# A two-stage kernel (attention, then a capacity mixture of experts): first steps reordered, row stores held for the next norm, and the seventh expert's list moved up

## The chip, the cores and the metric

The kernel runs on one core of a Trainium2 chip. The metric is device time in microseconds (us) of one execution, the median of several runs. The profile is one execution recorded by the hardware profiler; its engines are PE (TensorE's matmuls, with PEld for its weight loads), DVE (VectorE), ACT (ScalarE), POOL (GpSimd) and SP (SyncE, which issues most transfers).

## The reference

Eight batches of eight heads, 576 positions, head size 64. Heads 0 to 3 look at the last 32 positions, heads 4 to 7 at every 32nd. The rows of all heads side by side are the tokens of a mixture of eight experts, each of which takes at most 576 tokens: the pairs (token, expert) are served from the largest logit down.

```python
scores = scale * np.matmul(q, k.transpose(0, 1, 3, 2))
masks = np.stack([mask_local if h < H // 2 else mask_strided for h in range(H)], axis=0)
scores = np.where(masks[None, :, :, :], scores, -1000000000.0)
attn = np.exp(scores - np.max(scores, axis=-1, keepdims=True))
attn = attn / (np.sum(attn, axis=-1, keepdims=True) + 1e-09)
x = np.matmul(attn, v)                      # (B, H, S, D) -> x: (4608, 512)
logits = x @ w_gate                         # (4608, 8)
for idx in np.argsort(-logits.flatten()):   # largest first
    tok, e = (int(idx) // E, int(idx) % E)
    if assigned[tok] >= 0 or counts[e] >= cap:
        continue
    assigned[tok] = e
    counts[e] += 1
for e in range(E):
    mask = assigned == e
    out[mask] = np.maximum(x[mask] @ w1[e], 0.0) @ w2[e]
```

## The kernel before

**Attention.** Work is cut into 16 units: for each batch one with the four strided heads (even units) and one with the four local heads (odd units). A unit has two parts, of two heads each, and each part is one step, so there are 32 steps, i = 0 to 31. In the body of the loop over i, step i finishes the scores of the part behind it (`close_scores`), turns the rows of the part before it (`turn`), multiplies the part's own weights by the values in two halves (`mix(p, 0)`, `mix(p, 1)`, 36 or 24 matmuls each) into the one accumulator `po`, opens the scores of the part after next (`open_scores`), scales its rows (`norm`), and shifts and exponentiates the scores of the next part (`shift`). Between the two halves stands `max_t`, which turns the maxima and makes `dd` on DVE. The order of the lines is the order on each engine: this stage has no scheduler, and every engine serves its queue strictly in order.

Local units need their values twice, shifted by 32 rows: `copy_v` copies rows in SBUF, six copies a unit. `square_v` sums the squares of a batch's values on ACT; `total_v` (a matmul with `twos` and a sum on DVE) and `scale_v` make of it a power of two by which rows are scaled in `norm`. For the first unit the scale comes too late, so `rescale` applies it afterwards.

Loads go out on SP through `flow`: a load waits for the third last one before it, or for a mark (a unit's `top` or its last norm, `done`). `load_kq` brings the keys and queries of one part, `load_v` half of a unit's values. `store` writes a unit's rows to `x_scr` in DRAM, one unit and a half behind; strided units use six transfers, three on SP and three on POOL.

**Experts.** A search on DVE and PE finds each expert's threshold in turn (`side`). For expert number ph (0 to 7), `weights` loads w1 and w2, sums their squares (`jk`, L990) and splits them into two halves of 16 bits (w1h, w1l, w2h, w2l, L1008 and L1009); `slots` numbers its tokens; `close` and `take` remove them from the logits, and prepare the next search (`point`); `fetch` makes the list of its rows: one-hot rows on DVE (`ohh`, `ohl`, `rv`), 36 small matmuls (L951), two more (L959), `idx`, then five gathers on POOL (`xr`, L1068), halving on ACT and DVE (`xg`) and five transposes by transfer (`xt`, L1059). `ffn` runs the first layer (192 matmuls of 288 columns, L1163), then the second in tiles of 128 tokens, the first, the tail tile of 64 (L1205) and three more (L1211). Each tile's rows are written by an indirect transfer on POOL (L1222).

Here PE's order is written by a clock of estimated costs: `chains` holds generators that say how long to wait before their next piece, and pieces are issued among the matmuls when the clock reaches their time. For the other engines a scheduler orders by priority; `urgent` raises it. `HURRY` names the experts whose one-hot rows are urgent, `T_HOT` is the wait between these rows and the 36 matmuls, `T_F` one ahead of a list.

## Time and profile before

| | |
|---|---|
| median of 3 runs | 682.43 us (677.96 to 693.18) |
| the profiled execution | 682.75 us, span 681.0 us |
| PE busy | 603.8 us, 89% of the span |
| DVE busy | 459.7 us, 68% |
| ACT busy | 330.9 us, 49% |
| POOL busy | 112.4 us, 16% |
| mean granted TensorE clock | 0.958 of full |
| moved by transfers | 102.40 MB, mean 150 GB/s |

The share of busy time is an average over stages with different limits: attention until about 190 us, the first search until about 225, then the experts. A busy PE is not PE at its peak, since matmuls overlap in the record: in a row of 24 matmuls at full rate each shows more than the distance to the next one. Idle time of an engine counts only where that engine is waited for.

### The profile page before, as it was taken

Reading aid. Unit: us, or ns where it says so; the run is one execution under the profiler, and the core shown is the slowest. Engines: PE = TensorE matmul, PEld = TensorE weight load, DVE = VectorE, ACT = ScalarE, POOL = GpSimd, SP = SyncE. Lnnn points to the kernel's source line nnn. Section 1 sums busy time; section 2 is a strip of 40 time slices with the busy share of each in tenths; the row PEclk is TensorE's granted clock in tenths of the full one; section 3 lists DMA queues with packets and bytes.
Section 4 is the critical chain, followed back from the end, with each engine's and each line's share of the span. In section 5 each row is a group of like instructions: output and inputs, shape, how many; then the busy total and the mean of one; then the engine's idle time right before and its main releaser. Section 6 shows DMA issues by size and latency. Waiting matters only on the chain.

```text
span 681.0 us, 19420 instructions
## 1 busy us (share of the span) xinstructions
PE 603.8 (89%) x8125; PEld 396.3 (58%) x8128; DVE 459.7 (68%) x1388; ACT 330.9 (49%) x551; POOL 112.4 (16%) x124
## 2 busy tenths in 40 slices
PE   8799999898946699889989999989989996999993
PEld 4576766776633475476467458447537644746741
DVE  4767887787877887787686686787777746580200
ACT  2444664446302564843851771673574386771210
POOL 2011101111001100500420430240150041211011
PEclk9779999899976899999999999999999997999997
DMA  8968888787414505913930860870680386911010
GB/s 239 215 168 248 237 241 235 184 249 213 126 38 171 163 9 184 243 31 117 261 80 30 302 125 1 284 173 2 222 203 33 134 258 192 248 35 47 1 39 31
DMA packets 76363, 102.40 MB, mean 150 GB/s; under 512 B 41292, under 2 KB 49062, under 8 KB 75763
## 3 DMA queue, kind: packets, MB, share of 16 engines
q1 hardware_dynamic: 68195, 79.61, 41.4%
q0 software_dynamic: 7360, 21.15, 10.3%
q8 instruction: 64, 1.05, 0.7%
q10 hardware_dynamic: 720, 0.39, 0.2%
q14 instruction: 24, 0.20, 0.1%
HBM read 73.60 MB, written 18.87 MB: 136 GB/s over the span
## 4 chain that ended last, share of the span: by engine, by line
PE 22%; issue 14%; DVE 11%; DMA 10%; ACT 5%; POOL 4%; SPq 1%; POOLq 0%; DVEq 0%; ACTq 0%
PE ph L1163 17%; DMA w<-in_w_dram 6%; POOL xr L1068 2%; DMA xt<-xg 2%; DMA xr<-x_scr,idx 2%; PE ph L1211 2%; DVE w1l L1009 2%; POOL out_dram L1222 1%; ACT jk L990 1%; DVE w2l L1009 1%; DVE xg L1058 1%; ACT w1h L1008 1%; DVE hl L1171 1%; DVE cm L807 1%; ACT xg L1057 1%
## 5 line engine op out<-in xcount | busy, mean ns | idle before, releaser
L1163 PE MATMUL ph<-xt,w1h 128*128 128x288 f16 (+2 forms) x1024 | 177.7, 289 | 9.1 <-DMA xt<-xg 6.7
L1163 PEld LDWEIGHTS <-w1h 128*128 128x128 f16 x1024 | 97.4, 99 | 40.2 <-issue 7.7
L1163 PE MATMUL ph<-xt,w1l 128*128 128x288 f16 (+2 forms) x512 | 111.5, 288 | 0.0
L1222 POOL DMA_INDIRECT out_dram<-y,idx x40 | 50.6, 1265 | 332.0 <-ACT y L1221 304.8
L1211 PE MATMUL ph<-w2h,hh 128*128 128x512 f16 x256 | 97.0, 379 | 1.3 <-DVE hl L1171 1.3
L1170 ACT ACTIVATE hh<-ph 128x576 f16<-128x576 f32 (+2 forms) x72 | 42.7, 595 | 113.4 <-PE ph L1163 113.2
L990 ACT ACTIVATE jk<-w 128x1024 f16<-128x1024 f32 x64 | 67.5, 1054 | 61.3 <-DMA w<-in_w_dram 60.0
L1211 PE MATMUL ph<-w2h,hl 128*128 128x512 f16 x256 | 97.0, 379 | 0.0
L1211 PE MATMUL ph<-w2l,hh 128*128 128x512 f16 x256 | 96.9, 379 | 0.0
L1171 DVE SCALAR_TENSOR_TENSOR hl<-ph,hh 128x576 f16<-128x576 f32 (+2 forms) x72 | 49.5, 687 | 49.1 <-ACT hh L1170 49.1
L1211 PEld LDWEIGHTS <-hh 128*128 128x128 f16 x512 | 49.2, 98 | 57.2 <-issue 6.6
L1163 PEld LDWEIGHTS <-w1l 128*128 128x128 f16 x512 | 50.4, 99 | 14.1 <-issue 1.3
L374 ACT ACTIVATE pr<-spa 128x576 f32<-128x576 f32 x32 | 20.8, 651 | 63.2 <-PE spa L371 51.2
L1068 POOL DMA_INDIRECT xr<-x_scr,idx x40 | 41.8, 1046 | 54.9 <-DMA w<-in_w_dram 25.3
L1009 DVE SCALAR_TENSOR_TENSOR w1l<-w,w_sw,w1h 128x512 f16<-128x512 f32 x64 | 45.4, 744 | 6.4 <-ACT w1h L1008 6.4
L1009 DVE SCALAR_TENSOR_TENSOR w2l<-w,w_sw,w2h 128x512 f16<-128x512 f32 x64 | 46.4, 744 | 1.8 <-ACT w2h L1008 1.6
L1211 PEld LDWEIGHTS <-hl 128*128 128x128 f16 x256 | 24.9, 97 | 38.7 <-issue 13.4
L1008 ACT ACTIVATE w1h<-w,w_sw 128x512 f16<-128x512 f32 x64 | 42.4, 708 | 3.1 <-DVE w_sw L208 1.8
L1008 ACT ACTIVATE w2h<-w,w_sw 128x512 f16<-128x512 f32 x64 | 41.2, 710 | 5.7 <-DVE w_sw L208 5.7
L1221 ACT ACTIVATE y<-ph,so 128x512 f32<-128x512 f32 x32 | 21.8, 680 | 44.3 <-PE ph L1211 31.7
L425 POOL DMA_DIRECT2D x_scr<-xs x23 | 15.0, 659 | 161.0 <-DVE vsum L296 113.1
L1058 DVE TENSOR_TENSOR xg<-xr,xg 128x512 f16<-128x512 f32 (+1 forms) x37 | 25.3, 687 | 14.8 <-ACT xg L1057 14.6
(618 smaller groups left out, 932.5 us busy)
## 6 DMA issues: line engine op xcount, KB each, us to landing
w<-in_w_dram SPq DMA_DIRECT2D x64, 512.0 KB
kl<-in_kl_dram SPq DMA_DIRECT2D x16, 304.0 KB
v_s<-in_ns_dram SPq DMA_DIRECT2D x16, 292.5 KB
v_l<-in_nl_dram SPq DMA_DIRECT2D x16, 292.5 KB
ks<-in_ks_dram SPq DMA_DIRECT2D x16, 288.0 KB
qs<-in_qt_dram SPq DMA_DIRECT2D x16, 288.0 KB
ql<-in_qt_dram SPq DMA_DIRECT2D x16, 288.0 KB
x_scr<-xl SPq DMA_DIRECT2D x8, 512.0 KB
```

The source lines that it names most:

```text
L374: nc.scalar.activation(pr[:, :S].rearrange("k (h n) -> k h n", h=2), u.sp[p][:, :, :HS], AF.Exp, scale=0.125)
L990: nc.scalar.activation(jk, wf[:, c * n4:(c + 1) * n4].rearrange("p c f -> p (c f)"), AF.Square, scale=1.41422, accum_out=sq[:, c:c + 1])
L1008: nc.scalar.activation(hi[:, c, f], wf[:, c, f], AF.Copy, scale=s_)
L1009: nc.vector.scalar_tensor_tensor(lo[:, c, f], wf[:, c, f], s_, hi[:, c, f], op0=OP.mult, op1=OP.subtract)
L1058: nc.vector.tensor_tensor(xs[:, 1], xv, xs[:, 0], op=OP.subtract)
L1068: nc.gpsimd.indirect_dma_start(out=xr[:n], out_offset=None, in_=x_rows, in_offset=bass.IndirectOffsetOnAxis(ap=idx[:n, t:t + 1], axis=0))
L1163: nc.tensor.matmul(tile_[:, j, :w], wt[:, d, f * 128:(f + 1) * 128], xt[:, d // 2, xx, d % 2, c], start=(k == 0), stop=(k == 3 * DC - 1))
L1170: nc.scalar.activation(hv, src, AF.Relu)
L1171: nc.vector.scalar_tensor_tensor(lv, src, 0.0, hv, op0=OP.max, op1=OP.subtract)
L1211: nc.tensor.matmul(py, a[:, f, ts_], w[:, f], start=(k == 0), stop=(k == len(todo) - 1))
L1221: nc.scalar.activation(y, py, AF.Copy, scale=so[:, t:t + 1])
L1222: st = nc.gpsimd.indirect_dma_start(out=out_rows, out_offset=bass.IndirectOffsetOnAxis(ap=idx[:n, t:t + 1], axis=0), in_=y[:n], in_offset= ...
```

## The change

Four things are changed in attention. The three copies of unit 1 within the odd row blocks (`k % 2`) run on ACT instead of DVE. The Square of units 1 and 2 is issued behind the `shift` of steps 1 and 2, and `total_v` with `scale_v` of the first two batches stands between the two halves of the mix of steps 2 and 4, instead of behind the `shift` of steps 1 and 3; the copies and the Square of unit 3 and the `rescale` move behind the work of their step (`late`). The keys and queries of unit 2 are loaded ahead of its values, without marks. And the first SP store of a unit waits for the last norm of the next unit, as the POOL stores did before.

For the seventh expert (ph = 6) the one-hot rows are urgent, the list starts without `T_F` and its matmuls after 3200 instead of 4200 of the planner's nanoseconds, `close` comes 9000 later, and of `close` only the three pieces are run that the eighth expert needs, which takes all tokens that are left.

```diff
-HURRY = (0, 1, 7)
+HURRY = (0, 1, 6, 7)
+T_HOT6, T_CLOSE6 = 3200, 9000
@@ copy_v
-                if k % 2:
+                if k % 2 and u is todo[1]:
+                    nc.scalar.activation(vn[64:96, t], vn[32:64, t], AF.Copy)
+                elif k % 2:
@@ store
-                            if q is nc.gpsimd and u not in todo[-3:]:
+                            if (q is nc.gpsimd or SR * f + k == 0) and u not in todo[-3:]:
                                 wait_for(ins, todo[todo.index(u) + 1].done)
...
-                    nc.sync.dma_start(xs[:n, :4 * D].rearrange("(t q) f -> q t f", q=128), xo[:, :n // 128])
+                    ins = nc.sync.dma_start(xs[:n, :4 * D].rearrange("(t q) f -> q t f", q=128), xo[:, :n // 128])
+                    if u not in todo[-3:]:
+                        wait_for(ins, todo[todo.index(u) + 1].done)
@@ the tables of the steps
-        mids2, mids3 = {1: todo[1]}, {}
-        squares = {}
+        mids2, mids3 = {2: todo[1]}, {}
+        squares, behind = {}, {-1: todo[0].square_v}
...
-                squares.setdefault(1, []).append(u.square_v)
+                behind[1] = u.square_v
                 for p in range(2):
-                    drips.setdefault(2, []).append(lambda p=p: todo[0].rescale(p))
+                    late.setdefault(2, []).append(lambda p=p: todo[0].rescale(p))
...
-                        q, o = (late, -4) if j == 3 and k % 2 else (drips, COPY_AT[k])
+                        q, o = (late, -3) if j == 3 and k in (0, 1, 3, 5) else (drips, COPY_AT[k])
...
-                    squares.setdefault(2 * j - V_AT + 2, []).append(u.square_v)
+                    (late if j == 3 else squares).setdefault(2 * j - V_AT + 2, []).append(u.square_v)
@@ the first loads
-        for f in range(2):
-            todo[2].load_v(f)
+        for p in range(2):
+            todo[2].load_kq(p)
+            todo[2].load_v(p)
@@ the loop over the steps
+            if i in (2, 4):
+                mids2[i].total_v(b)
+                mids2[i].scale_v()
...
-            if i in mids2 and i > 1:
+            if i in mids2 and i > 4:
                 mids2[i].total_v(b)
             warm(i, 3)
-            if i == -1:
-                todo[0].square_v()
-            if i == 1:
-                todo[1].total_v(b)
-                todo[1].scale_v()
+            if i in behind:
+                behind[i]()
@@ indices, side
-        yield T_HOT1 if ph == 1 else T_HOT
+        yield T_HOT1 if ph == 1 else T_HOT6 if ph == E - 2 else T_HOT
...
-            chains.append([due_now() + (T_F if 1 < ph < E - 1 else 0), fetch(ph, slot, wts)])
+            chains.append([due_now() + (T_F if 1 < ph < E - 2 else 0), fetch(ph, slot, wts)])
+            if ph == E - 2:
+                yield T_CLOSE6
...
-                    for f in todo:
+                    for f in todo if ph < E - 2 else todo[:3]:
```

**VectorE in steps 1 and 2.** Before, from the maxima of unit 1's first part on (`mx_l_141`); `v_l_143` are unit 1's values, `mr`, `mh` and `dd` the chain from the maxima to the shift.

```order
L352 TENSOR_REDUCE mx_l_141<-spa 128x18
L324 COPY v_l_143<-v_l_143 32x780 x3
L361 TENSOR_REDUCE mr<-spa 64x32
L363 TENSOR_TENSOR mh<-mr 64x32
L364 TENSOR_TENSOR mh<-mr,mh 64x32
L366 TENSOR_TENSOR dd<-mh,bm 128x576
L404 TENSOR_SCALAR rc_407<-po 118x12
L407 RECIPROCAL rc_407<-rc_407 118x12
L409 TENSOR_TENSOR xs<-po,rc_407 118x2x6x64
L296 TENSOR_REDUCE vsum<-spb 128x1
```

After the change, from the same row on.

```order
L355 TENSOR_REDUCE mx_l_141<-spa 128x18
L364 TENSOR_REDUCE mr<-spa 64x32
L366 TENSOR_TENSOR mh<-mr 64x32
L367 TENSOR_TENSOR mh<-mr,mh 64x32
L369 TENSOR_TENSOR dd<-mh,bm 128x576
L407 TENSOR_SCALAR rc_404<-po 118x12
L410 RECIPROCAL rc_404<-rc_404 118x12
L412 TENSOR_TENSOR xs<-po,rc_404 118x2x6x64
L330 COPY v_l_143<-v_l_143 32x780 x2
L330 COPY v_l_143<-v_l_143 32x520
L355 TENSOR_REDUCE mx_l_145<-spa 128x18
```

The three copies of L324 have left the engine, and the six small operations on the batch's scale that began with `vsum` (L296) stand only behind the next part's `dd`.

**TensorE in step 2.** Before, from the second shift matmul of step 1 on; `twos` is the weight of `total_v`, `vsq_113` the sums of squares of the first batch, L391 the mix, L358 the turned maxima.

```order
L371 MATMUL spa<-dd,sel 128x288
L294 LDWEIGHTS twos
L294 MATMUL spb<-vsq_113,twos 128x2
L348 MATMUL spa<-ql,kl 64x32 x24
L391 MATMUL po<-v_l_143,pr_127 32x65 x18
L358 MATMUL spa<-ident,mx_l_145 32x64 x2
L391 MATMUL po<-v_l_143,pr_127 32x65 x18
```

After the change:

```order
L374 MATMUL spa<-dd,sel 128x288
L351 MATMUL spa<-ql,kl 64x32 x24
L394 MATMUL po<-v_l_143,pr_127 32x65 x18
L361 MATMUL spa<-ident,mx_l_145 32x64 x2
L295 LDWEIGHTS twos
L295 MATMUL spb<-vsq_113,twos 128x2
L394 MATMUL po<-v_l_143,pr_127 32x65 x18
```

The matmul of the total has gone from ahead of the scores and the mix into the middle of the mix, and the second half of the mix is queued behind it.

**GpSimd at the seventh expert.** Before: the gathers of the sixth expert's rows (`xr`), outputs, the gathers of the seventh, outputs.

```order
L1068 DMA xr<-x_scr,idx 128x512 x4
L1068 DMA xr<-x_scr,idx 64x512
L1222 DMA out_dram<-y,idx 4608x512 x5
L1068 DMA xr<-x_scr,idx 128x512 x4
L1068 DMA xr<-x_scr,idx 64x512
L1222 DMA out_dram<-y,idx 4608x512 x3
```

After the change:

```order
L1078 DMA xr<-x_scr,idx 128x512 x4
L1078 DMA xr<-x_scr,idx 64x512
L1234 DMA out_dram<-y,idx 4608x512 x4
L1078 DMA xr<-x_scr,idx 128x512 x4
L1078 DMA xr<-x_scr,idx 64x512
L1234 DMA out_dram<-y,idx 4608x512 x4
```

The seventh expert's gathers stand ahead of one output, that of the tail tile. On TensorE the 36 list matmuls of this expert stand behind four matmuls of the sixth expert's tail tile; before, they stood behind all 24 and eight of the next tile. The transposes and weight loads on SP keep their order but for the read of the eighth expert's number, which now stands behind the first transpose of the seventh.

## Rows read from the trace of the kernel before

**Rows 1.** Stretches: start:end, length, busy (instructions) of each engine, PEclk, DMA share, GB/s.

```profile
core 0: us, PE busy (x) PEld busy (x) DVE busy (x) ACT busy (x) POOL busy (x), PEclk, DMA share, GB/s
16.20:22.48 6.28, 4.18 (x138) 3.26 (x130) 5.22 (x17) 2.86 (x3) 0.00 (x0) 1.00 0.88 166
22.48:31.89 9.41, 6.70 (x139) 4.52 (x133) 8.11 (x22) 2.54 (x4) 0.00 (x0) 0.73 1.03 237
31.89:40.57 8.68, 7.11 (x147) 5.55 (x147) 3.84 (x11) 4.95 (x8) 2.18 (x3) 0.70 0.87 228
40.57:47.51 6.94, 6.94 (x153) 5.83 (x152) 4.25 (x15) 2.45 (x6) 0.00 (x0) 0.76 0.37 96
47.51:61.81 14.30, 13.80 (x425) 9.96 (x423) 11.58 (x31) 9.53 (x16) 0.56 (x1) 1.00 0.85 239
194.00:214.00 20.00, 10.63 (x224) 7.86 (x222) 15.69 (x66) 0.00 (x0) 0.00 (x0) 0.50 0.10 33
```

**Rows 2.** Timeline, steps 1, 2: start, length, engine, instruction; idle time before, and releaser.

```profile
17.61 1.51 DVE L324 COPY v_l<-v_l 32x780 f32<-32x780 f32 x3 [0.40 <-DMA v_l<-in_nl_dram]
...
19.29 2.12 ACT L291 ACTIVATE jk<-v_l 64x2304 f16<-64x2304 f32 x1 [3.14 <-DVE v_l L324]
...
20.35 0.41 PE L371 MATMUL spa<-dd,sel 128*128 128x288 bf16 x2 [1.13 <-DVE dd L366]
...
21.55 0.16 PE L294 MATMUL spb<-vsq,twos 128*128 128x2 bf16 x1 [0.80 <-ACT jk L291]
...
28.64 0.32 PE L348 MATMUL spa<-qs,ks 64*54 64x54 f32 x8 [1.59 <-DMA qs<-in_qt_dram]
```

**Rows 3.** Timeline of step 7: a unit's stores on SP and the next norm.

```profile
59.65 1.81 SPq L425 DMA_DIRECT2D x_scr<-xs  x3
...
60.13 0.82 DVE L409 TENSOR_TENSOR xl<-po,rc 128x640 f32<-128x640 f32 x1
```

**Rows 4.** Stretches where the seventh expert takes over.

```profile
540.00:550.00 10.00, 9.50 (x88) 4.54 (x86) 6.02 (x31) 7.07 (x13) 2.00 (x2) 1.00 0.97 349
550.00:560.00 10.00, 10.00 (x48) 4.51 (x46) 5.43 (x8) 8.38 (x14) 6.21 (x7) 1.00 0.76 211
562.54:567.85 5.31, 0.28 (x2) 0.10 (x2) 4.70 (x12) 4.45 (x9) 1.74 (x2) 0.84 0.94 220
567.85:573.20 5.35, 5.35 (x24) 3.32 (x25) 1.62 (x3) 0.63 (x2) 0.00 (x0) 0.52 0.88 348
```

**Rows 5.** Timeline: the rows of the sixth and the seventh expert.

```profile
500.61 7.58 SPq L1059 DMA_TRANSPOSE xt<-xg  x5
...
511.08 0.65 PE L1163 MATMUL ph<-xt,w1h 128*128 128x288 f16 x4
...
541.92 1.05 PE L1205 MATMUL ph<-w2h,hh 128*64 128x512 f16 x8
...
543.40 1.02 DVE L943 TENSOR_TENSOR ohl<-sh,iota 128x768 f16<-128x768 f16 x2
...
546.47 1.32 PE L951 MATMUL pr__8784<-ohl,rv 128*32 128x64 f16 x36
...
550.37 0.98 POOL L1068 DMA_INDIRECT xr<-x_scr,idx  x1 [0.31 <-issue]
...
555.99 7.99 SPq L1059 DMA_TRANSPOSE xt<-xg  x5
...
567.85 0.90 PE L1163 MATMUL ph<-xt,w1h 128*128 128x288 f16 x3 [4.11 <-DMA xt<-xg]
```

**Rows 6.** Timeline of the seventh expert's first layer: the eighth's list.

```profile
574.08 0.76 DVE L1171 SCALAR_TENSOR_TENSOR hl<-ph,hh 128x576 f16<-128x576 f32 x1 [4.61 <-ACT hh L1170]
...
580.25 1.51 PE L951 MATMUL pr__9136<-ohl,rv 128*32 128x64 f16 x36 [1.55 <-DVE rv L937]
```

**Rows 7.** The tile `xr`, 545 to 575: from issue to landing, five gathers.

```profile
DMA to landing us min/median/max: 3.4/3.6/3.8
```

More of the change, by code (lines that the diff above doesn't have):

```diff
@@ L558, in band_stride_attention_then_capacity_moe @@
                     for k in range(6):
-                        q, o = (late, -4) if j == 3 and k % 2 else (drips, COPY_AT[k])
+                        q, o = (late, -3) if j == 3 and k in (0, 1, 3, 5) else (drips, COPY_AT[k])
                         q.setdefault(2 * j + o, []).append(lambda u=u, k=k: u.copy_v(k))
-                    squares.setdefault(2 * j - V_AT + 2, []).append(u.square_v)
+                    (late if j == 3 else squares).setdefault(2 * j - V_AT + 2, []).append(u.square_v)
                 else:
-                    squares.setdefault(2 * j - V_AT_S + 1 + (j == 2), []).append(u.square_v)
+                    if j == 2:
+                        behind[2] = u.square_v
+                    else:
+                        squares.setdefault(2 * j - V_AT_S + 1, []).append(u.square_v)
                 if not u.strided:
-                    mids2[2 * j - 3] = u
-                    drips.setdefault(2 * j - 2, []).append(u.scale_v)
+                    mids2[2 * j - 3 + (j == 3)] = u
+                    if j > 3:
+                        drips.setdefault(2 * j - 2, []).append(u.scale_v)
             if not u.strided and u.b < B - 1:
@@ L618, in band_stride_attention_then_capacity_moe @@
             nu_ = todo[i // 2 + 3] if i >= 0 and i // 2 + 3 < nu else None
-            kq_ = todo[i // 2 + 2] if i >= 0 and i // 2 + 2 < nu else None
+            kq_ = todo[i // 2 + 2] if i >= 2 and i // 2 + 2 < nu else None
             if nu_ and i % 2 == 0:
```

## The prediction

> **What bounds the kernel now.** The profiled execution took 682.75 us: a span of 681.0 and 1.75 around it. The sum below is made against it; it stands 0.3 above the median of the three runs, 682.43. I read three views, in the order of the change's parts: a table of stretches over the first attention steps, then the timeline inside two of them, then the same two views where the seventh expert takes over from the sixth.
>
> *The first steps.* [Rows 1] is cut where steps 1 to 5 begin their first mix. Steps 5 to 7 take 14.30 us together, 4.77 each, at full clock. Steps 1 to 4 take 6.28, 9.41, 8.68 and 6.94: 1.5, 4.6, 3.9 and 2.2 more, 12.2 in all. Three things share this. In step 1 VectorE does three row copies (1.51) ahead of the maxima, so TensorE waits 1.13 for `dd`; then the `total` matmul waits 0.80 for ScalarE's Square, which itself had to wait for the copies [rows 2]. In step 2 TensorE waits 1.59 for unit 2's query [rows 2]. And the granted clock is 0.73, 0.70 and 0.76 over steps 2 to 4 [rows 1], a mix of full rate and half (2.4 and 1.2 GHz). The DMA share is 0.87 to 1.03 until 40.57 and 0.37 behind it [rows 1]: the loads are nearly a second bound, and have slack only in step 4, where TensorE is slow.
>
> *The hand-over.* TensorE ends the sixth expert at 562.54, is busy for 0.28 of the next 5.31 us, and then runs 24 matmuls in 5.35 at a mean clock of 0.52 [rows 4]. The wait is 4.11 on the transposed tokens `xt` [rows 5]. Its chain backwards: transposes issued from 555.99 on, the gather on POOL from 550.37 on, and the 36 list matmuls at 546.47, which stand behind the whole tail tile (from 541.92) and eight more matmuls, though the one-hot rows were ready at 544.42 (543.40 + 1.02) [rows 5].
>
> **The change, part by part.**
>
> *Step 1.* The three copies move to ScalarE. No copy on it is in the trace. A Square of 2304 elements takes 2.12 there [rows 2], 0.92 ns an element, so one of 780 takes 0.72 from below; from above it is the whole 2.12. I take 0.85, close to the row's slope: from 17.6, when `v_l` has landed [rows 2], to 20.2. VectorE's chain to `dd` runs 1.5 earlier, the exponential behind it only from 20.2 on, against 21.5 when it followed the Square. Step 2 begins 1.3 earlier. At 2.12 a copy it begins later than now by some 2.5.
>
> *Steps 2 to 4.* TensorE's work in a step at full rate is its busy time by the mean clock: 6.70 x 0.73 = 4.9, 7.11 x 0.70 = 5.0, 6.94 x 0.76 = 5.3 [rows 1]. To this come waits. Step 2 loses the one for the query (unit 2's keys and queries are now ahead of its values) and the rescale, which goes behind the norm; it gains one, since `total` now stands between the two halves of the mix and its Square (2.12) begins only after the exponential: 0.5 of TensorE's time, and the second half, masks and next scores queue behind it. With 0.8 for the maxima that is 6.2. Step 3: 0.6 of waits, 5.6. Step 4: `total` of the second batch waits in the same place for unit 3's Square, which waits for four copies (0.5 each by [rows 2]) and the Square: 2.0 of waits, 7.3. Sum 19.1 against 25.0: 5.9, and 1.3 of step 1: 7.2. Off this I take 1.5 for one spell at half clock of some 3 us, since TensorE still idles about 1 us in steps 2 and 4, and 0.7 for late loads: **5.0**. The loads give a bound of their own: until 47.51 the DMA engines are idle for 0.13 x 8.7 + 0.63 x 6.9 = 5.5 [rows 1], so the same bytes cannot be down much more than 5.5 sooner. From above: 8.0, if some loads are not yet needed and the clock holds; from below 0.
>
> *Row stores.* The first store on SP now waits for the next unit's norm of the same step. Before, it went out at 59.65 while that norm ended at 60.95 (60.13 + 0.82) [rows 3]: 1.3 later at most. Behind it on SP stand the next values, whose copies are due more than a step (4.8) later, and the loads after those wait for a later norm anyway. Nobody reads a stored row before the experts. I cost it at nothing, hidden by that lead; without it, up to 1.3 in a step, and in the other direction as much, since loads get the engines first.
>
> *The seventh list.* The 36 matmuls now stand behind four tail matmuls, near 542.5. VectorE's list, with four operations of the close dropped, is ready about 543.5 instead of 544.42, so TensorE waits some 0.3 inside the tail. From these matmuls to the gather it is 3.9 now (550.37 - 546.47); about 0.9 of that is the tail's output, a POOL transfer like the 0.98 of the gather's first, and that now goes behind the gather. So the gather starts near 542.7 + 3.0 = 545.7 instead of 550.37: 4.7 sooner. On ScalarE the first halving waits for a Square and the tail's copy until about 550, and the transposes start near 551.3, 4.7 sooner too. They are ready 11.86 later, as now (567.85 - 555.99), at 563.2, or 10.5 later, as for the sixth expert (511.08 - 500.61, where TensorE has no wait named) [rows 5], at 561.8. TensorE arrives at 562.54 + 0.3. Against now that saves 4.95 of the start, and the first 24 matmuls, which at full rate take 5.35 x 0.52 = 2.8 [rows 4] save 2.55: 7.5.
>
> Then the eighth list is next late: TensorE waits 1.55 for VectorE's `rv` now, at 580.25 [rows 6]. VectorE's part before it begins with the first `hl`, at 574.08 [rows 6]. Ahead of that stand the first five splits of w2, which now run inside the stall. Their scale comes no sooner than before, near 564.5, since w1's splits and Squares fill ScalarE until then; five at 0.76, the price of that `hl`, end near 568.3. So this chain comes 5.8 sooner and TensorE 7.5: the wait grows by 1.7, and 5.8 are left. I take **5.5**, 0.3 off for a little lost clock behind a wait of 3 us. Bounds: 7.5, and 1.5 if the rows come late. The eighth expert's weights, gather and later close have the seventh's first layer as cover, 192 matmuls or 8 times the 2.8 above; without it each us late is one us.
>
> Sum: 682.75 - 5.0 - 0 - 5.5 = 672.25, **672**.
>
> **Rivals.**
>
> *Both in full*: clock holds, lists meet: 8.0 and 7.5, 667.3. For it: steps 5 to 7 hold full clock at TensorE 13.80 of 14.30 [rows 1]. Against it: the new waits of steps 2 and 4, and `rv`.
>
> *The loads set the pace*: step 4's scores need unit 3's keys, which stand behind two units' values; the first steps give 1 and the list 5.5, 676. For it: shares of 0.87 and more until 40.57; against it 0.37 behind [rows 1].
>
> *The rows come late*: the gather moves from a stretch with a DMA share of 0.76 into one of 0.97 and 349 GB/s [rows 4], where the seventh expert's weights land. If its rows came only with the last weights, about 551 to 553, ScalarE, which serves in order, would push halvings and splits by some 4: the list gives 1.5, the sum 676. Against it: a gather landed in 3.4 to 3.8 us in the old place [rows 7]. The Trainium skill's page DMA: Bandwidth & Descriptors, section Issuing engines are not separate DMA queues, says that transfers started by any engine run on the same 16 engines and interleave; by that rule this rival holds, at least in part, and the sum is 676 and not 672. No row of before shows the gather beside the weights.
>
> *Neither takes hold*: the waits only move; 681.
>
> *Slower, the clock*: from 194 to 214 TensorE is busy 10.63 of 20 us and stays at 0.50 throughout [rows 1]. If the shorter waits of steps 2 to 4 leave it as thin, it stays at half through step 7: six steps of 2 x 4.6 (13.80 / 3) from 21 on end at 76, against 61.8 now, +14; with 5.5 of the list that is 691. It decides from four such steps on (21 + 37 = 58 where step 6 starts at 52.7: +5.3, which the list cancels). Against it: each spell of the first steps ended, and the stretch from 47.51 shows 1.00.
>
> **How the numbers follow.** Forecast 0.40 (own range 669 to 675), both in full 0.24, loads 0.14, late rows 0.12, neither 0.05, slower 0.05. 663 to 678 leaves out neither and slower, and what noise adds. Over 2% (about what a measurement of this kernel can tell from no change) is below 668.8: both in full, and a little of the forecast's low end, 0.28. Above 696 it needs the clock and more: 0.03. Within: 0.69.
>
> **What would show it.** Right: step 6's first mix near 47.7 instead of 52.70; no wait for `qs` in step 2; the clock of steps 2 to 4 above 0.8; waits of 0.5 and 1.3 on `total`; the gather at 545.6; no wait over 0.5 for `xt` at the seventh expert, and full clock behind it; a wait of about 3 for `rv`. Wrong: copies of over 1.2 on ScalarE, `v_l` of unit 3 landing after 31, halvings that start behind 552, or a mean clock below 0.7 from 21 to 45.

## The result, and the profile after

The changed kernel takes 678.87 us (median of 22 runs, 672.02 to 685.47); the kernel before, in the runs beside it, 686.11 (677.96 to 694.44). The ratio is 0.9885, with an interval of 0.986 to 0.991: about 1.15% faster, within the 2% that the forecast called no change. On the 682.75 that the forecast was worked against, this ratio gives 674.9; the forecast was 672. The other part of the distance is the level: over 22 runs the kernel before has a median 3.7 above the 682.43 of the three runs shown. Ratios, and the means of profiles below, are formed from undisturbed runs alone; four profiles, marked * in the table, are of disturbed ones. A ratio is loose: set against the kernel before three more times, the same changed kernel gave 0.9898, 1.0014 and 0.9856 (below).

The profiled execution after has a span of 674.4, against 681.0, a gain of 6.6. It does not come evenly. Step 8's first mix starts at 60.36 (before 61.81): 1.45 sooner. The first expert's first layer starts at 220.36 (225.59): 5.23. The sixth expert ends at 560.27 (562.54): 2.27. The last matmul's group ends at 663.08 (669.71): 6.63.

The first steps, in the table of stretches, cut where steps 1 to 6 and step 8 begin their first mix; they answer to [rows 1]:

```profile
core 0: us, PE busy (x) PEld busy (x) DVE busy (x) ACT busy (x) POOL busy (x), PEclk, DMA share, GB/s
16.29:21.40 5.11, 4.03 (x136) 3.11 (x129) 4.28 (x11) 3.06 (x5) 0.00 (x0) 1.00 0.62 178
21.40:26.79 5.39, 4.18 (x134) 2.97 (x134) 4.71 (x18) 2.79 (x3) 0.00 (x0) 1.00 0.92 208
26.79:32.95 6.16, 4.99 (x146) 3.60 (x145) 4.91 (x14) 3.81 (x7) 1.33 (x2) 1.00 0.99 213
32.95:43.52 10.57, 8.33 (x154) 6.63 (x153) 6.03 (x20) 4.90 (x8) 1.24 (x2) 0.64 1.00 270
43.52:51.24 7.72, 7.72 (x149) 5.48 (x148) 3.85 (x10) 3.81 (x7) 0.00 (x0) 0.61 0.57 173
51.24:60.36 9.12, 8.62 (x278) 6.09 (x276) 7.70 (x21) 5.93 (x10) 0.56 (x1) 1.00 0.74 206
```

Steps 1 to 3 run at full clock, and step 4 begins 7.62 us sooner than before. Then steps 4 and 5 take 18.29 us instead of 12.13, at a mean clock of 0.63, and only 1.45 is left. The timeline shows where the clock breaks (start, length, engine, instruction; idle time before, and releaser):

```profile
18.29 2.34 ACT L325 ACTIVATE v_l<-v_l 32x780 f32<-32x780 f32 x3 [2.06 <-DMA v_l<-in_nl_dram]
...
21.40 0.76 PE L394 MATMUL po<-v_l,pr 64*32 64x65 f32 x36 [0.91 <-ACT pr L377]
...
23.59 0.16 PE L295 MATMUL spb<-vsq,twos 128*128 128x2 bf16 x1 [0.94 <-ACT jk L292]
...
32.95 0.89 PE L394 MATMUL po<-v_s,pr 64*54 64x65 f32 x24
...
33.60 2.12 ACT L292 ACTIVATE jk<-v_l 64x2304 f16<-64x2304 f32 x1 [1.08 <-DVE v_l L327]
...
35.84 0.71 ACT L458 ACTIVATE xt<-spb 128x384 f32<-128x384 f32 x2
...
36.38 0.16 PE L295 MATMUL spb<-vsq,twos 128*128 128x2 bf16 x1 [1.78 <-ACT xt L458]
36.48 1.55 PE L394 MATMUL po<-v_s,pr 64*54 64x65 f32 x24
```

The second batch's `total` (L295) waits 1.78 us in the middle of step 4. It is let go not by the Square but by the copies of L458, which read the bank (a part of the matmuls' result memory) that `total` is to write, and which stand behind the Square on ScalarE. The second 24 mix matmuls, behind this wait, take 1.55 us, at half rate; the first 24, at 32.95, took 0.89.

The hand-over to the seventh expert, in the timeline (it answers to [rows 5, 6]):

```profile
540.78 1.50 PE L961 MATMUL pr__8723<-ohl,rv 128*32 128x64 f16 x36
...
543.74 0.98 POOL L1078 DMA_INDIRECT xr<-x_scr,idx  x1 [0.84 <-DVE idx L973]
...
550.13 0.63 ACT L1067 ACTIVATE xg<-xr 128x512 f16<-128x512 f32 x1 [3.45 <-DMA xr<-x_scr,idx]
...
551.55 8.63 SPq L1069 DMA_TRANSPOSE xt<-xg  x5
...
563.33 0.54 PE L1175 MATMUL ph<-xt,w1h 128*128 128x288 f16 x3 [2.92 <-DMA xt<-xg]
...
563.70 3.17 ACT L1018 ACTIVATE w2h<-w,w_sw 128x512 f16<-128x512 f32 x5 [0.82 <-DVE w_sw L209]
...
564.46 3.40 DVE L1019 SCALAR_TENSOR_TENSOR w2l<-w,w_sw,w2h 128x512 f16<-128x512 f32 x5 [0.33 <-ACT w2h L1018]
...
567.78 0.75 DVE L1183 SCALAR_TENSOR_TENSOR hl<-ph,hh 128x576 f16<-128x576 f32 x1
...
573.85 1.50 PE L961 MATMUL pr__9134<-ohl,rv 128*32 128x64 f16 x36 [1.95 <-DVE rv L947]
```

The list and the gather are as early as forecast. But ScalarE then waits 3.45 for the rows, `xt` still costs TensorE 2.92 (4.11 before), and `rv` 1.95 (1.55 before). The clock behind the wait for `xt` stays full, as forecast: the first three matmuls take 0.54 us, against 0.90 before.

### The profile page after: what moved, and what is told of

Its sections match the earlier page's. It is cut to its first block, busy times and chain, and to the rows that moved or that the text cites. A ratio compares the mean times of both kernels' runs of the same rounds, so it can differ in the third digit from the quotient of the medians.

```text
span 674.4 us, 19427 instructions
## 1 busy us (share of the span) xinstructions
PE 602.9 (89%) x8125; PEld 394.4 (58%) x8128; DVE 456.9 (68%) x1381; ACT 333.0 (49%) x554; POOL 110.8 (16%) x124
## 4 chain that ended last, share of the span: by engine, by line
PE 46%; issue 16%; DVE 15%; DMA 11%; ACT 6%; POOL 3%; SPq 1%; another core or an unknown queue 0%; POOLq 0%; ACTq 0%; DVEq 0%
PE ph L1175 17%; PE ph L1223 7%; PE po L394 4%; PE spa L351 4%; DMA w<-in_w_dram 4%; DMA xr<-x_scr,idx 2%; DVE w2l L1019 2%; DVE w1l L1019 2%; POOL xr L1078 2%; ACT jk L292 2%; DMA v_s<-in_ns_dram 2%; POOL out_dram L1234 1%; PE spb L469 1%; PE spa L374 1%; ACT w1h L1018 1%
## 5 line engine op out<-in xcount | busy, mean ns | idle before, releaser
L1234 POOL DMA_INDIRECT out_dram<-y,idx x40 | 47.8, 1195 | 337.2 <-ACT y L1233 314.6
L428 POOL DMA_DIRECT2D x_scr<-xs x23 | 16.5, 724 | 154.0 <-DVE vsum L297 101.4
L394 PE MATMUL po<-v_s,pr 64*54 64x65 f32 x768 | 31.3, 230 | 2.4 <-DMA v_s<-in_ns_dram 1.5
```

Of the source, the lines that this page charges most:

```text
L394: nc.tensor.matmul(po[r:r + u.nq, j - j0], pr[k, o:o + u.nq], u.vn[k, t, 2 * p + h], start=(j == j0), stop=(j == j1 - 1), skip_group_check ...
L1234: st = nc.gpsimd.indirect_dma_start(out=out_rows, out_offset=bass.IndirectOffsetOnAxis(ap=idx[:n, t:t + 1], axis=0), in_=y[:n], in_offset= ...
```

## Experiments

### What can be read from one run

Beside the ratios, each kernel's profile gives three stretches that scatter far less than the whole: where step 4 and step 8 begin their first mix, and the time from the end of the sixth expert's second layer to the end of the eighth's. The stretch between them, from the first expert's first layer to the sixth expert's end, was edited in no kernel but for its last 25 us (the seventh list), and still took 335.5 to 344.4 us; this scatter is a large part of what makes a ratio loose. All in us; "half" is the time at half clock within steps 4 and 5, 2 x (1 - mean granted clock) x length, from clocks of two digits and so good to some 0.2.

| kernel | first steps | list | step 4 at | steps 4+5 | half | step 8 at | from 6th's end |
|---|---|---|---|---|---|---|---|
| before | old | old | 40.57 | 12.13 | 3.4 | 61.81 | 107.17 |
| e2_list | old | new | 41.83 | 11.19 | 1.1 | 62.13 | 104.01 |
| e3_store * | old | old | 42.18 | 11.43 | 1.6 | 62.72 | 105.76 |
| f1_no_first | old | new | 40.62 | 10.87 | 0.0 | 60.60 | 103.18 |
| after | new | new | 32.95 | 18.29 | 13.5 | 60.36 | 102.81 |
| e8_same | new | new | 34.42 | 16.48 | 13.5 | 60.35 | 102.78 |
| f4_same | new | new | 33.38 | 18.35 | 13.6 | 60.84 | 102.92 |
| g4_same * | new | new | 35.99 | 16.56 | 10.3 | 61.67 | 103.78 |
| e1_first | new | old | 34.40 | 15.91 | 6.7 | 59.81 | 106.22 |
| f2_no_store | new | new | 32.98 | 15.42 | 3.4 | 58.22 | 103.12 |
| f3_no_list * | new | old | 37.91 | 16.66 | 10.3 | 63.68 | 105.31 |
| e4_total | edited | new | 32.65 | 17.03 | 10.2 | 58.80 | 103.71 |
| e5_warm | edited | new | 34.78 | 15.06 | 0.0 | 59.70 | 102.82 |
| e10_fill | edited | new | 36.76 | 13.56 | 2.4 | 59.43 | 105.21 |
| e7_hold * | new | edited | 32.53 | 17.42 | 10.1 | 59.06 | 109.18 |
| e11_hold2 | new | edited | 34.25 | 17.36 | 13.9 | 60.72 | 103.24 |
| g1_slots | new | edited | 34.61 | 13.14 | 0.5 | 57.81 | 108.99 |
| e9_both | edited | edited | 34.85 | 19.28 | 6.8 | 63.66 | 109.71 |
| e12_fill_hold | edited | edited | 33.05 | 13.59 | 0.0 | 57.04 | 104.78 |
| g2_fill_slots | edited | edited | 32.53 | 16.37 | 3.3 | 58.83 | 109.46 |

### One part alone

e1_first is the kernel before with the new first steps alone:

```diff
-        mids2, mids3 = {1: todo[1]}, {}
+        mids2, mids3 = {2: todo[1]}, {}
...
+            if i in (2, 4):
+                mids2[i].total_v(b)
+                mids2[i].scale_v()
```

> The kernel before with the first attention steps alone in the new order (copies on ScalarE, other load order, unit 3's copies and the two totals moved); row stores and the seventh list as before. My theory, from the trace of the changed kernel: step 5 begins about 4 us sooner, but behind the wait of 1.78 us for the second total in step 4 the clock stays at half for some 13 us and gives most of it back, so that step 8 begins only 1 to 2 us sooner. The ratio is 0.998 (0.995 to 1.000). Rival, the forecast's own size of 5.0 us: 0.9925. Rival, the same 5 us, as the shift of 5.2 us at the first expert in the one profiled execution has it: 0.9925 too, with the gain coming after step 8.

Measured: ratio 0.9952 (0.9912 to 0.9993). e2_list is the kernel before with the list alone:

```diff
-HURRY = (0, 1, 7)
+HURRY = (0, 1, 6, 7)
...
-                    for f in todo:
+                    for f in todo if ph < E - 2 else todo[:3]:
```

> The kernel before with the seventh expert's list alone moved ahead. My theory, from the trace of the changed kernel: the rows land in some 6 us instead of 3.6 beside the weights, TensorE still waits about 3 us for xt but at full clock behind it; the gain is 4 to 5.5 us, ratio 0.993 (0.991 to 0.995). Rival, rows come as late as the forecast's rival had it: 1.5 us, 0.998. Rival, the forecast's term in full without a longer wait for rv: 7.5 us, 0.989.

Measured: ratio 0.9993 (0.9960 to 1.0027), but 104.01 from the sixth expert's end on, 3.2 less than before. e3_store is the kernel before with the stores alone:

```diff
-                            if q is nc.gpsimd and u not in todo[-3:]:
+                            if (q is nc.gpsimd or SR * f + k == 0) and u not in todo[-3:]:
```

> The kernel before with the row stores alone held behind the next unit's norm. My theory: nobody waits for a stored row, and the loads behind it on the queue are due more than a step later; ratio 1.000 (0.997 to 1.003). Rival, the loads get the engines first and the later attention steps gain: 0.995 or less. Rival, the loads behind the store come late: 1.004 or more.

Measured: 1.0039 (0.9990 to 1.0087). Neither a gain nor a loss can be told. The three ratios make 0.998 together where the whole has 0.9885; by ratios the parts do not add.

### One part taken out, and the changed kernel again

f1_no_first, f2_no_store and f3_no_list are the changed kernel with the lines of one of the diffs above (and what belongs to them) put back; e8_same, f4_same and g4_same are the changed kernel itself.

> The changed kernel with the first attention steps put back into the old order; stores and list stay changed. The parts alone gave 3.3, 0.5 and -2.7 us by their ratios, 1.1 us in sum, while the whole gives 7.8 and 6.9; here each part is taken out of the whole. Theory, the parts add and the ratios of the parts alone were off by their spread: step 8 begins 2.4 us later, ratio 0.992 to 0.9935. Rival, the parts need each other: without the new first steps hardly anything is left, 0.998 or more.

> The changed kernel with the row stores as before; first steps and list stay changed. Theory, the stores cost and bring nothing: 0.989 (0.986 to 0.992). Rival, the new first steps gain only if the stores stand back from the loads: then step 8 begins 2 us later or the steps after it lose, and the ratio is 0.995 or more.

> The changed kernel with the seventh list at its old place; first steps and stores stay changed. Theory, by the stretch from the end of the sixth expert to the end (106.4 us in the mean of three profiles with the old list, 103.2 in the mean of five with the new one): 3.2 us of the gain go, ratio 0.9935. Rival, the list gives nothing, as its ratio alone had it (0.9993): 0.989. Rival, it gives the 5.5 forecast: 0.9965.

> The changed kernel once more without an edit, as the measure for the three beside it: 0.9885 to 0.990, step 8 near 60, 102.8 us from the end of the sixth expert on.

> The changed kernel without an edit, a second profiled execution on this chip, to see which waits and half-clock spells are the kernel's own and which an execution's. Theory: the wait on the second total in step 4 (1.8 us) with a spell of 10 us or more behind it, the wait for xt (2.9) and that for rv (2.0) stand again within 0.5, and step 8 begins within 1 us of 60.4; ratio 0.9885 (0.986 to 0.991). Rival: the spell in steps 4 and 5 was that execution's, and is under 5 us here.

> The changed kernel once more without an edit, beside the two: steps 4 and 5 16 to 18.4 us with a half-clock spell, 102.8 from the sixth expert's end.

Measured: without the first steps 0.9947 (0.9902 to 0.9992), without the stores 0.9905 (0.9863 to 0.9947), without the list 0.9956 (0.9915 to 0.9997). The changed kernel itself: f4_same 1.0014 (0.9948 to 1.0080; medians 674.58 and 678.40), e8_same 0.9898 (0.9840 to 0.9955), g4_same 0.9856 (0.9783 to 0.9930). The spread of one kernel's own ratio is as wide as what these experiments look for, so the parts are read from the stretches.

The means leave out the profiles marked *; the figures in brackets have them in. Old first steps (three profiles): step 4 begins at 41.00 in the mean, step 8 at 61.52. New ones, not edited (seven): 33.86 and 59.73. So **the new first steps are 7.1 us ahead at step 4 and 1.8 at step 8** (7.0 and 1.6). Between, steps 4 and 5 take 16.42 instead of 11.40, with 9.3 us at half clock instead of 1.5. Whether the 1.8 stays cannot be told: the first expert starts at 218.9 instead of 221.7 in the mean, but single profiles have it from 215.3 to 225.6. Old list (two): 106.70 from the sixth expert's end on; new list, not edited (nine): 103.40. So **the list gives 3.3 us** (2.7). In sum 5.1 us (4.3). The first ratio says 7.9 (6.1 to 9.6); what lies between is not settled by these runs.

Whether the spell in steps 4 and 5 belongs to the kernel: it stands in nine of the ten profiles with the new first steps unedited (six of the seven without a mark), but its length differs, 3.4 to 13.9 us. In seven of the nine it begins inside the wait on `total` or within 1.7 us behind it; in e8_same and e11_hold2 it had begun before, behind waits of 1.89 and 1.14 in step 3. Two profiles show the length best. f2_no_store and the changed kernel agree on TensorE to 0.03 us from 32.98 to 39.35, the wait of 1.78 included. Here are the stretches behind that wait, first of the changed kernel, then of f2_no_store:

```profile
36.38:39.35 2.97, 2.96 (x52) 2.21 (x51) 2.13 (x10) 0.17 (x1) 0.00 (x0) 0.50 1.00 343
39.35:42.45 3.10, 3.10 (x66) 2.47 (x62) 0.21 (x1) 1.83 (x3) 0.00 (x0) 0.50 1.03 230
42.45:49.73 7.28, 7.28 (x104) 5.04 (x100) 4.22 (x10) 3.40 (x5) 0.00 (x0) 0.52 0.53 153
```

```profile
36.38:39.35 2.97, 2.97 (x51) 2.21 (x51) 2.13 (x10) 0.17 (x1) 0.00 (x0) 0.52 1.10 371
39.35:42.32 2.97, 2.97 (x78) 2.35 (x74) 0.94 (x2) 1.97 (x4) 0.00 (x0) 0.91 0.98 245
42.32:48.40 6.08, 5.40 (x150) 3.98 (x148) 3.94 (x11) 3.71 (x7) 0.00 (x0) 1.00 0.72 192
```

The clock falls at 36.5 in f2_no_store and at 35.8 in the changed kernel. In f2_no_store it is back after 3.4 us, in the other it stays at half for 10 us more of a TensorE that is busy all the time. Step 8 begins at 58.22 and at 60.36.

### The wait in step 4

e4_total moves the second `total` behind the second half of the mix:

```diff
-            if i in (2, 4):
+            if i == 2:
...
             warm(i, 2)
+            if i == 4:
+                mids2[i].total_v(b)
+                mids2[i].scale_v()
```

> The changed kernel with one edit: the total of the second batch stands in step 4 behind the second half of the mix and the next scores' first part, ahead of the norm, and no longer between the halves. My theory, the wait breaks the clock: the 1.78 us wait shrinks below 0.5, the half-clock spell of 13.6 us behind it is gone or under 4 us, and step 8's first mix comes 4 to 7 us sooner than in the changed kernel; ratio to the kernel before 0.979 to 0.983 instead of 0.9885. Rival, the loads are the bound: steps 5 to 7 then wait for unit 4's keys and values, since the DMA engines are busy at a share of 0.9 and more until 43; at most 2 us sooner, 0.9855. Rival, the clock falls in these steps whatever the order: a spell of the same length stands a step later, 0.9885.

Measured: 0.9865 (0.9806 to 0.9924). The wait on `total` is gone, and two others stand near its place:

```profile
34.24 0.31 PE L361 MATMUL spa<-ident,mx_s 128*32 128x64 f32 x4 [0.70 <-DVE mx_s L355]
...
37.47 0.32 PE L351 MATMUL spa<-ql,kl 64*64 64x32 f32 x8 [1.33 <-issue]
```

Behind them the clock is at half for 10.2 us again, and steps 4 and 5 take 17.03. So one wait less does not do it. e5_warm and e10_fill leave the wait and give TensorE idle matmuls (fillers, whose results nobody reads) in front of `total`: e5 eight in step 4, in total's own bank `b`; e10 eight in step 4 and four in step 2, in the next scores' bank `a`, which is free. The lines of e10:

```diff
+                for _ in range(8 if i == 4 else 4):
+                    nc.tensor.matmul(a[:, 0, :512], warm_i[:, :128], warm_i, start=True, ...)
                 mids2[i].total_v(b)
```

> The changed kernel with eight idle matmuls of 512 columns (about 0.22 us each at full rate) on TensorE in step 4, between the first half of the mix and the second total; no other edit. Theory, the wait costs the clock: the wait for ScalarE stays as long, but TensorE is busy in it, the half-clock spell of 13.6 us behind it is gone, and step 8's first mix comes 4 to 6 us sooner, near 55; ratio to the kernel before 0.980. Rival, the loads set the pace: TensorE then waits for unit 3's queries or unit 4's values, and step 8 begins at most 2 us sooner; 0.986. Rival, the clock falls for the thin work of these steps and not for this one wait: the spell stays and the eight matmuls cost nothing, 0.9885.

> The changed kernel with idle matmuls of 512 columns on TensorE ahead of the second matmul of each total: four in step 2, eight in step 4, this time written into the bank of the next scores, which is free there (in the run before they stood in the total's own bank, whose last reader is the copy that the total itself waits for, and so ran behind the wait and not in it). Theory, the 1.8 us wait in step 4 breaks the clock and the half-clock spell behind it (3.4 to 13.7 us long in seven of eight profiles with the new first steps) takes the gain back: with TensorE busy in the wait there is no spell from 33 to 50, steps 4 and 5 together take 13 us instead of 16.9 in the mean, and step 8's first mix stands near 56.5 instead of 60.3. Rival, the clock falls for all of the thin work of steps 2 to 4: a spell stands there again and step 8 is at 59 or later. Rival, without the spell the loads are late: a wait for kl, ql or v_s of 1 us or more in step 4 or 5.

Measured: e5_warm 0.9948 (0.9907 to 0.9988). Its filler missed the wait: it waited for the bank just as `total` does, and then cost 1.72 us of its own:

```profile
38.45 1.89 PE L661 MATMUL spb<-warm_i 128*128 128x512 bf16 x8 [1.77 <-ACT xt L458]
40.17 0.17 PE L295 MATMUL spb<-vsq,twos 128*128 128x2 bf16 x1
```

That the clock still held behind it (half 0.0) shows, with g1_slots (half 0.5, none of it behind its wait of 1.49), that the wait does not bring the spell every time. e10_fill: 0.9873 (0.9834 to 0.9912), no wait on `total`, steps 4 and 5 in 13.56. A short spell there (35.8 to 39.3) stands behind a wait of 2.33 in step 3 for which the profile names no releaser (see the last section). In e12_fill_hold (below) no such wait stands ahead: the filler fills the time in which `total` waited, no half clock before 99 us, step 6 at 46.64 (forecast 47.7) and step 8 at 57.04:

```profile
34.53 0.30 PE L361 MATMUL spa<-ident,mx_s 128*32 128x64 f32 x4 [0.59 <-DVE mx_s L355]
34.77 1.90 PE L661 MATMUL spa<-warm_i 128*128 128x512 bf16 x8
36.62 0.16 PE L295 MATMUL spb<-vsq,twos 128*128 128x2 bf16 x1
36.71 0.89 PE L394 MATMUL po<-v_s,pr 64*54 64x65 f32 x24
```

So the mechanism, a wait of TensorE and half clock behind it, is shown: of 18 waits of over 1 us that begin at full clock between 26 us and step 6 in the sixteen profiles with new first steps, edited or not, 16 have the clock fall inside them or within 2.2 us behind; no spell there begins without one, and e12_fill_hold has neither wait nor spell. That filling is worth a certain number of us of the whole is not shown.

### The hand-over

e7_hold lets the four loads of the seventh expert's w2 wait until its gather has landed; e11_hold2 only the last two. From e11_hold2:

```diff
-            fetch_w(range(k))
+            fetch_w(range(2 if ph == E - 2 and name == "w2" else k))
...
+                ins = held.pop()(range(2, 4))
+            tc.add_manual_dep(ins[0].ins, got.ins.name, ...)
```

> The changed kernel with one edit: the seventh expert's four loads of w2 (2 MB) wait until its last gather has landed, so that the rows come beside no more than the end of w1's loads; by this ScalarE also serves the halvings ahead of w2's Squares. Theory, the rows come late because of the weights: the first row block lands within 4 us of its issue instead of 6.4, xt is ready 3 us sooner, the wait of 2.92 us at the seventh expert's first layer falls below 0.5, of which the wait for rv takes back about 1; the stretch from the end of the sixth expert to the end, 102.8 us in the changed kernel, takes 101, ratio 0.986. Rival, the landing takes 6 us here whatever runs beside it: the wait for xt stays above 2 and the stretch at 102.8 or more. Rival, w2 now comes late in turn: the wait is moved to the second layer, 104 and more, 0.990.

> The changed kernel with the last two of the seventh expert's eight weight loads (1 MB of 4) held until its last gather has landed. Holding all four loads of w2 brought the rows in 3.3 us but made the scale of w2 7 us late; half of it held should cost nothing, since those two Squares came late on ScalarE anyway. Theory, rows beside weights are the cause of the late xt and, through ScalarE and VectorE, of the late rv: rows land in 4 to 5 us, the waits for xt and rv together take 3 us instead of 4.9 and the stretch from the sixth expert's end to the end 101.5 instead of 103.2. Rival, rv has a floor of its own (VectorE's w2 splits): the wait for xt goes, the one for rv grows by as much, 103.2. Rival, the scale of w2 is late again: 104 and more.

Measured in e7_hold: the first rows are used 3.3 us after the gather's issue instead of 6.4, and then TensorE waits 7.05 for the scale of w2, whose loads now come too late:

```profile
544.68 0.98 POOL L1081 DMA_INDIRECT xr<-x_scr,idx  x1 [1.32 <-DVE idx L973]
...
548.00 0.63 ACT L1070 ACTIVATE xg<-xr 128x512 f16<-128x512 f32 x1 [1.54 <-DMA xr<-x_scr,idx]
...
568.46 0.19 PE L1011 MATMUL pr__8962<-ss,ones_b 128*128 128x1 bf16 x1 [7.05 <-DVE ss L1009]
```

It takes 109.18 from the sixth expert's end on; no ratio was formed. e9_both (below), which has the same edit, agrees: rows used after 3.3, a wait of 6.69 for w2's scale, 109.71. In e11_hold2 the rows land in 3.6 us by the tile's view, and yet nothing is gained (103.24; ratio 0.9832, 0.9775 to 0.9889, an interval that overlaps those of the changed kernel itself):

```profile
DMA to landing us min/median/max: 3.5/3.6/3.7
```

```profile
562.76 0.18 PE L1011 MATMUL pr__8962<-ss,ones_b 128*128 128x1 bf16 x1 [0.85 <-DVE ss L1009]
...
564.75 0.54 PE L1183 MATMUL ph<-xt,w1h 128*128 128x288 f16 x3 [1.42 <-DMA xt<-xg]
...
575.85 1.50 PE L961 MATMUL pr__9134<-ohl,rv 128*32 128x64 f16 x36 [2.53 <-DVE rv L947]
```

0.85, 1.42 and 2.53 make 4.8, as 2.92 and 1.95 do in the changed kernel. In nine of the ten profiles with the new list and an unedited hand-over, `xt` and `rv` together take 4.3 to 5.3 however they are shared (1.26 and 4.00 in e2_list, 3.21 and 1.12 in e4_total; in the tenth, e10_fill, 3.57 and a wait of 1.66 for w2's scale): what TensorE gains at `xt` it gives back at `rv`. g1_slots moves the count behind `rv` ahead of the w2 splits:

```diff
...
+            if ph == E - 1:
+                slot = yield from slots(ph, *src, code, mv)
+            while ph >= 2 and ph - 2 not in emitted:
+                yield None
             wts = weights(ph, ei)
-            slot = yield from slots(ph, *src, code, mv)
+            if ph < E - 1:
+                slot = yield from slots(ph, *src, code, mv)
```

> The changed kernel with one edit in the planner: the slot count of the eighth list is written before that expert's weights and no longer behind them, so that VectorE does it (scan, slots, one-hot rows, rv) ahead of the seventh expert's five w2 splits instead of behind them. Theory, the floor under the seventh list's gain is this chain (w2's scale, five splits of 0.68, then 6.1 us to the list): the wait for rv, 1.1 to 4.3 us in all profiles of the new list, falls below 0.5, and the stretch from the sixth expert's end to the end takes 100 to 101.5 instead of 103.2. Rival, w1's last splits and w2's splits, pushed back by the 3 us of the list, make TensorE wait at the first or second layer instead: 103 or more. Rival, the wait for xt is what bounds: it stays, and rv's wait was only its rest, 103.2.

Measured: 1.0046 (1.0010 to 1.0081), 108.99. The list stands at 569.68, 7.5 behind the sixth expert's end instead of 13.6, and TensorE does not wait for it. It waits right behind it, and then for the eighth expert's scale:

```profile
569.68 1.30 PE L961 MATMUL pr__9097<-ohl,rv 128*32 128x64 f16 x36
...
573.56 0.20 PE L969 MATMUL pr__9141<-pick,p 128*64 128x10 f16 x2 [1.86 <-DVE p L964]
...
587.44 0.16 PE L1008 MATMUL pr__9243<-ss,ones_b 128*128 128x1 bf16 x1 [4.79 <-DVE ss L1006]
```

On ScalarE the last Square of the eighth's w1 begins at 586.06, behind three halvings that wait 1.93, 3.05 and 1.48 for that expert's rows: the early list has put the eighth gather (from 574.52) beside its weights (on SP from 564.69 to 576.46), as the change did to the seventh. So it is VectorE's order that sets the floor under `rv`, and taking it away costs more one expert later.

### Two edits together

e9_both joins e7_hold's edit and e5_warm's, e12_fill_hold those of e11_hold2 and e10_fill, g2_fill_slots those of g1_slots and e10_fill.

> Both edits together, the eight idle matmuls in step 4 and the loads of w2 held behind the gather. Theory: the two add, since they lie 500 us apart: 0.980 and 0.986 against 0.9885 make 0.9775. Rival, neither wait was worth its length, because the next one stands close behind: 0.987 or more.

> Both edits together: the idle matmuls in steps 2 and 4 and the last two weight loads held. Theory: step 8 near 56.5 and 101.5 from the sixth expert's end, 5.5 us below the changed kernel, ratio to the kernel before 0.981. Rival, neither holds: as the changed kernel, 0.989.

> The same edit, and the idle matmuls in steps 2 and 4. Theory: steps 4 and 5 take 13.6 us, and the stretch from the sixth expert's end 100 to 101.5; 4 to 5 us below the changed kernel, ratio to the kernel before 0.982. Rival: 0.9885, as the changed kernel.

Measured: 1.0003 (0.9969 to 1.0036), 0.9915 (0.9873 to 0.9956) and 1.0027 (0.9994 to 1.0061). The best first steps of all, 2.7 ahead of the mean in e12_fill_hold, come with 104.78 from the sixth expert's end on (waits of 2.46 for w2's scale, 1.21 for `xt`, 1.30 for `rv`). In e9_both steps 4 and 5 take 19.28: a wait of 2.48 for the maxima, e5's wait of 1.77, and the filler itself at half clock (3.4). No version was shown to beat the changed kernel.

## Why the prediction was wrong, step by step

**The sum.** The forecast took 10.5 us off; the first ratio says 7.9, the stretches 5.1 (4.3 with the marked profiles). Direction and place of both terms were right; both were too large.

**Step 1 and the copies: right.** Forecast 0.85 a copy from 17.6 to 20.2; the three take 2.34, 0.78 each, from 18.29 (`v_l` landed 0.7 later) to 20.63. Step 2 begins 1.08 sooner; forecast 1.3.

**Steps 2 and 3: right.** 5.39 and 6.16, forecast 6.2 and 5.6. The wait for the query is gone. The first `total` waits 0.94, forecast 0.5. Step 4 begins 7.6 sooner, forecast 7.6 (1.3 + 3.2 + 3.1).

**Step 4: here the first term failed.** Its waits were right (0.46 and 1.78, forecast 2.0 in all), if by the bank and not by the Square alone. Wrong was what follows: "I take 1.5 for one spell at half clock of some 3 us". The spell lasted 13.6 us here and 9.3 in the mean of seven profiles; steps 4 and 5, 13.1 us where the clock held (g1_slots), take 16.4 in the mean and 18.3 here. Forecast with its deduction was about 13.6 (7.3, 4.77 and the 1.5). So the spell was worth 3.3 to 5.2 and not 1.5, the two steps themselves take 1.1 more than forecast (13.1 against 7.3 + 4.77), and of the term's 5.0 only 1.8 is left at step 8. The forecast's sign for this, a mean clock below 0.7 from 21 to 45, did not come (0.81): steps 2 and 3 run at 1.00, and the spell reaches into step 5. The rival of the clock had the mechanism and expected it in every step; the forecast priced it from the short spells of [rows 1], and the row of 20 us at 0.50 that it had itself listed was the nearer one. The Trainium skill's page TensorE: Matmul & The Clock Gate, section HAM oscillation — how this bites in real kernels, has waits for transfers throw TensorE back to half rate, and the trace agrees, for a wait on ScalarE (1.78 of wait, then 0.50). Its section What's actually happening lets full rate come back once TensorE is busy. By that the spell would have been short; the rows above show 13 us of a TensorE that is always busy at half clock, and the measurement decides.

**The loads as a bound: fell.** After the wait for `v_s` at 12.45, which the kernel before has too, no row of the changed kernel shows TensorE waiting for an attention load itself up to 60 us. At one place a load holds it up through ScalarE: the 0.91 at 21.40 go back over the exponential and the three copies to `v_l`, which landed at 18.29.

**Row stores: right.** 1.0039 alone and 0.9905 without them; no effect that these runs can tell from nothing.

**The seventh list: the second term failed in two steps.** All times from the sixth expert's end. The gather was forecast at -16.8 and stands at -16.5. The halvings were forecast from -12.5 and begin at -10.1, since the rows take 6.4 us beside the weights and not 3.6 [rows 7]; the transposes come 2.5 late (-8.7, forecast -11.2), and `xt` at +3.1 instead of +0.3. That was the rival of the late rows, with 2.5 instead of the 4 it was priced at; e7_hold shows its cause. The Trainium skill's page DMA: Bandwidth & Descriptors, section Issuing engines are not separate DMA queues, has a gather and weight loads share the same engines, and the trace agrees: 6.4 us beside the weights, 3.3 without w2's. A sum between this rival's 676 and 672 would have been nearer.

The second is VectorE's chain to the eighth list, and it sets the end. The forecast had the five splits of w2 start near 564.5 (+2.0) and end at 568.3 (+5.8), by "Their scale comes no sooner than before, near 564.5". That was read too early: in the kernel before they start at +2.8 on ScalarE, and at +3.5 on VectorE, where they end at 569.47 (+6.9):

```profile
565.31 3.17 ACT L1008 ACTIVATE w2h<-w,w_sw 128x512 f16<-128x512 f32 x5 [0.86 <-DVE w_sw L208]
...
566.07 3.40 DVE L1009 SCALAR_TENSOR_TENSOR w2l<-w,w_sw,w2h 128x512 f16<-128x512 f32 x5 [0.33 <-ACT w2h L1008]
```

After the change they start at +3.4 and +4.2, and the first `hl` behind them at +7.5. Of the 1.7 that `hl` is later than forecast, 1.2 are this reading; 0.6 came with the change, perhaps because the late halvings push w1's splits on ScalarE, which no run isolates. The chain from `hl` to the list is 6.07, as in [rows 6] (6.17), and so the list stands at +13.6, forecast +11.9 (17.7 less 5.8). The list's place left the term 17.7 - 13.6 = 4.1; it measured 3.3 in the mean (4.4 in the profiled pair). Earlier rows did not help in e11_hold2, though its held loads cost 0.85 of their own.

**What the forecast left out.** From the first expert's start to the sixth's end the profiled pair differs by 2.96 against the change (336.95 and 339.91), all of it before the sixth expert starts, where the change touched nothing. From step 8 to the first expert it differs by 3.8 for the change (163.8 and 160.0); there the row stores lie, but with the old stores it takes as long (160.5 in f2_no_store).

## What to carry to other kernels

Price a wait on TensorE with the clock behind it, by the longest half-clock spell that the trace shows after a thin stretch and not by the shortest; a reordering that wins several us can hand them back a step later. When a transfer is moved earlier, look at what runs on the DMA engines at its new place, and follow the chain behind the next wait to its own floor before counting the saving. A wait without a releaser is worth a look at the queue that loads instructions. If runs scatter as much as the part is worth, compare stretches between fixed landmarks in several profiles rather than one ratio.

## What the runs showed of the hardware

The length of a half-clock spell does not follow from what the kernel's rows show: two executions (of the changed kernel and of f2_no_store, whose stores alone differ) that are alike on TensorE to 0.03 us through the 6.4 us around the wait were at half clock for 3.4 and for 13.5 us in these two steps. What sets the length stays open.

TensorE's waits without a releaser in the profile look random in time (1.89 before 32.27 in e8_same, 2.33 before 33.72 in e10_fill, none there in the changed kernel's first profile), but in the packed traces they stand at fixed places of its instruction stream. Of the 121 of over 0.25 us between 12 and 185 us in the twenty profiles, 118 stand every 256 instructions (weight loads counted), also where four fillers ahead have moved another matmul to that count. The traces also have a queue of the kind "instruction"; this is its line in the page after:

```profile
q8 instruction: 64, 1.05, 0.6%
```

These are 64 packets of 16 KB, as many as TensorE has blocks of 256 instructions (some 16,360). In all 118 waits the last of them had landed 1.2 to 1.8 us before TensorE went on (at 30.73 in e8_same, at 32.26 in e10_fill). So these waits, of 0.3 to 3.4 us, are for the next block of the program. What makes a packet late is not shown. Such a wait lay ahead of the half-clock spell in e8_same, e10_fill and e4_total (its 1.33).
